# The first sequence's strided attention: 18 rows a block on TensorE, three residues a group, two groups written at once

## Chip, core and metric

One NeuronCore of a Trainium2 chip (trn2). The metric is the device time of one execution in microseconds. The profiler gives, beside that, the span from the first to the last instruction and one row per instruction.

## What is computed

Strided and local causal attention over 4 sequences of 576 positions with 8 heads of 64, then a gated FFN and a maxout FFN over the 2304 tokens, all in fp32:

```python
rel = pos[:, None] - pos[None, :]
mask_local = (rel >= 0) & (rel < 32)                                     # heads 0 to 3
mask_strided = (rel >= 0) & (pos[None, :] % 32 == pos[:, None] % 32)     # heads 4 to 7
attn = softmax(where(mask, q @ k.T / 8, -1e9)) @ v                       # 4 x 8 x 576 x 64
x = attn as 2304 x 512
x = (silu(x @ w_gate) * (x @ w_val)) @ w_out                             # d_ff 1536
out = max(x @ w1, x @ w2, x @ w3) @ w_out2                               # d_ff 768
```

## The kernel before

**Tiling.** A row is 32 tokens, so a sequence has `NI` = 18 rows and the four have 72. They are cut into five chunks of 15, 15, 14, 14 and 14 rows (`ROWS`). The gated FFN runs a chunk at a time: for each of 12 slices f of d_ff a gate product (`emit_gate`), a value product (`emit_val`) and, one slot later, the output product (`emit_out`). A product takes three TensorE passes over a high and a low part (L503 to L505, 480 columns), and the output product of chunk 0 is one fp32 matmul (L549). `x` of a chunk, high and low part, lies in SBUF (`x_tile(c)`, L345 and L346 write it). The maxout FFN follows from about 560 us on.

**Attention.** In local attention a block of two rows sees itself and the row before. In strided attention a position sees only positions of its own residue modulo 32, so one residue of one sequence is a causal attention of 18 by 18. The kernel does it in two ways. On TensorE (`strided_block`): `ON_PE` holds, for a sequence, how many rows are done so and how many residues make a group; a group of 4 residues by 16 rows is a masked attention of 64 by 64, and a `Block` holds two groups. On VectorE or GpSimd (`Unit`): all 32 residues and 4 heads lie on 128 partitions, and a row's scores are an elementwise product with K (L415) and a sum (L418), its output a product with V (L437) and a sum (L440).

**A block** is loaded with three DMAs (L287 to L289), then scores (L299, or L303 outside the opening), a VectorE scan per group (L311), L314, exps on ScalarE (L316), L319 to L321, transposes (L326), their copy out of PSUM (L329 on ScalarE, for every third block L331 on VectorE), the product with V (L340), and, for each piece that `dst` yields, a write of the high part by ScalarE (L345) and of the low part by VectorE (L346). A strided block's `dst` yields one piece for each group and each chunk that its rows touch.

**The opening.** Before the FFN starts, the four strided blocks of the first sequence and four local blocks (rows 0 to 15) are done with tiles from the pool of weights (`wpool`, 35 tiles of 128 x 512). Loads of raw weights come after the blocks with index 2 and 7 (`RAW_AT`). Then eight steps of weight conversion (`LEADW`) are put out.

**Chunk 0's slots.** Each slot holds three steps of weight conversion: a load of a raw float64 weight (L147, 4 buffers), ScalarE (L158, L159), GpSimd (L160, L161), VectorE (L162, which frees the raw buffer, and L163), and a split into high (L135, ScalarE) and low (L138); value and output weights are also written to DRAM (L176) for the later chunks. `attention_steps(1)` puts the attention of chunk 1 into the same slots: the local blocks of rows 16 to 29, the four strided blocks of the second sequence (rows 0 to 11 of it), and, on VectorE, a unit of rows 16 and 17 of the first sequence, with its loads of K, V and q (L399, L400, L404). Chunk 2's attention, with a unit of rows 12 to 17 of the second sequence on GpSimd, begins three slots before chunk 1.

**Order.** The order on each engine is set at build time by a scheduler that simulates the kernel; every engine and SyncE's queue of DMA issues then run their instructions in that order. `silu` (L523) and exp (L316, L425) use different tables of ScalarE, so a change between them is an `ACT_TABLE_LOAD`.

Of the kernel before, what the change touches and what calls it, by code (L numbers as in the profile page):

```python
# [15 lines left out]
B, H, S, D = 4, 8, 576, 64  # L16
DM, DFF, DFF2 = 512, 1536, 768
NT = B * S
STRIDE = 32
NI = S // STRIDE  # L20

LR = 2
QB = LR * STRIDE
# [14 lines left out]
NC = len(ROWS) - 1  # L38
N = STRIDE * max(ROWS[c + 1] - ROWS[c] for c in range(NC))

ON_PE = [(0, 16, 4), (1, 12, 5)]

EARLY = -(-ROWS[1] // LR)

# [15 lines left out]
def tile_attention_swiglu_maxout(  # L60
# [48 lines left out]
    def f32(ap):  # L109
        return ap.bitcast(F32)  # L110


    cols = [128, KB, KB] + [n * r for _, n, r in ON_PE]
    cst = const.tile([128, sum(cols)], F32, name="cst")
# [3 lines left out]
    def width(c):  # L118
        return STRIDE * (ROWS[c + 1] - ROWS[c])

    def pieces(i0, i1):

        for c in range(NC):
            a, b = max(i0, ROWS[c]), min(i1, ROWS[c + 1])
            if a < b:
                yield c, a - ROWS[c], b - ROWS[c], a - i0
# [110 lines left out]
    def x_tile(c):  # L237
        if c not in xt:
            xt[c] = tuple(x_p.tile([128, NK, N], F32R, name=f"x{p}", tag=f"x{p}{c % 2}") for p in "hl")
        return xt[c]  # L240
# [4 lines left out]
    class Block:  # L245
# [86 lines left out]

        def pv(self):
            ps = self.bank()
            nu = self.nu
            for u in range(nu):
                for h in range(4):
                    a, j = divmod(h, 2)
                    m = (2 * u + a) * 128 + j * QB
                    nc.tensor.matmul(  # L340
                        ps[j * D:(j + 1) * D, (a * nu + u) * QB:(a * nu + u + 1) * QB], self.v[:, u, h],
                        self.pt[:, m:m + QB], start=True, stop=True,
                    )
            for hi, lo, src in self.dst(ps[:, :2 * nu * QB].rearrange("p (a m) -> p a m", a=2)):
                nc.scalar.activation(hi, src, AF.Copy)  # L345
                nc.vector.tensor_tensor(lo, src, f32(hi), ALU.subtract)  # L346

    def local_block(g, early=False):


        def dst(src):
            for c, i0, i1, o in pieces(LR * g[0], LR * (g[-1] + 1)):
                t, w = slice(i0 * STRIDE, i1 * STRIDE), slice(o * STRIDE, (o + i1 - i0) * STRIDE)
                xh, xl = x_tile(c)
                yield xh[:, 0:2, t], xl[:, 0:2, t], src[:, :, w]

        src = (earq if early else locq, lock, locv)
        return Block(src, (g[0] if early else g[0] - EARLY, g[0]), KB, [mask[0 if n % (NI // LR) == 0 else 1] for n in g], dst, early)

    def strided_block(srcs, b, g, early=False):  # L360

        _, rows, nr = ON_PE[b]

        def dst(src):
            for u, n in enumerate(g):
                r0 = min(n * nr, STRIDE - nr)
                su = src[:, :, u * QB:u * QB + nr * rows].rearrange("p a (r i) -> p a r i", i=rows)
                for c, i0, i1, o in pieces(b * NI, b * NI + rows):
                    def part(t):
                        t = t[:, 2:4, :width(c)].rearrange("p a (i r) -> p a r i", r=STRIDE)  # L370
                        return t[:, :, r0:r0 + nr, i0:i1]

                    xh, xl = x_tile(c)
                    yield part(xh), part(xl), su[:, :, :, o:o + i1 - i0]

        return Block(srcs, (g[0], g[0]), rows * nr, [smask[b]] * len(g), dst, early)

    def pairs(ns):
        ns = list(ns)
        return [ns[i:i + 2] for i in range(0, len(ns), 2)]  # L380

    class Unit:
# [28 lines left out]
        def qk(self, r, eng):  # L411
            i = self.i0 + r
            pr = pr_p.tile([128, NI * D], F32, name="pr")
            pv = pr[:, :(i + 1) * D].rearrange("p (j d) -> p j d", d=D)
            eng.tensor_tensor(  # L415
                pv, self.k[:, 0:i + 1, :], self.q[:, r:r + 1, :].to_broadcast([128, i + 1, D]), ALU.mult
            )
            nc.vector.tensor_reduce(self.sc[:, r, 0:i + 1], pv, AX.X, ALU.add)  # L418
# [14 lines left out]
        def pv(self, r, eng):  # L433
            i = self.i0 + r
            pr = pr_p.tile([128, NI * D], F32, name="pr")
            pv = pr[:, :(i + 1) * D].rearrange("p (d j) -> p d j", d=D)
            eng.tensor_tensor(  # L437
                pv, self.v[:, :, 0:i + 1], self.sc[:, r:r + 1, 0:i + 1].to_broadcast([128, D, i + 1]), ALU.mult
            )
            nc.vector.tensor_reduce(self.o[:, r], pv, AX.X, ALU.add)  # L440
# [20 lines left out]
    def attention_steps(c):  # L461
# [4 lines left out]
        blocks = [local_block(g) for g in pairs(g for g in range(-(-a // LR), -(-b // LR)) if g >= EARLY)]  # L466
        if a <= NI < b and len(ON_PE) > 1:
            blocks += [strided_block((st1q, st1k, st1v), 1, g) for g in pairs(range(-(-STRIDE // ON_PE[1][2])))]
        at = [0, 0, 4, 4, 8] if len(blocks) < 6 else [0, 0, 2, 2, 4, 4, 6, 6, 8]
# [6 lines left out]
        units = []  # L476
        on_pe = {n: rows for n, rows, _ in ON_PE}
        i = a
# [39 lines left out]
    def emit_gate(c, f):  # L518
        n = width(c)
        ps = gv.tile([128, 512], F32, name="ps_g", tag="gv")  # L520
        linear(ps[:, :n], wt["g", f], xt[c], n)
        t = h_p.tile([128, N], F32, name="ht", tag="ht" if c or f % 2 else "hh")[:, :n]
        nc.scalar.activation(t, ps[:, :n], AF.Silu)  # L523
        return t
# [227 lines left out]
    if True:  # L752
        blocks = [strided_block((st0q, st0k, st0v), 0, g, True) for g in pairs(range(-(-STRIDE // ON_PE[0][2])))]
        blocks += [local_block(g, True) for g in pairs(range(EARLY))]
# [30 lines left out]
        for s, (c, f) in enumerate(slots):  # L785
# [6 lines left out]
            t = emit_gate(c, f)  # L792
# [172 lines left out]
```

## Time and profile before

| | us |
|---|---|
| median of 3 runs | 852.14 |
| lowest, highest | 848.91, 855.87 |
| the profiled execution | 850.72 |
| its span, first to last instruction | 848.9 |
| TensorE busy in the span | 808.7 (95%) |
| VectorE, ScalarE, GpSimd busy | 519.3, 374.4, 408.7 |
| mean granted clock of TensorE | 0.986 of full |

Busy time is a mean over stages with different limits. A timeline row gives start, length, engine, line and, in brackets, how long the engine stood idle before it and what released it. PE is TensorE's matmul, DVE VectorE, ACT ScalarE, POOL GpSimd, SPq the queue of SyncE.

### The profile page before, as it was taken

The page shows a single profiled execution, that of the slowest core. Times are in us where ns is not written, and L with a number is a line of the kernel's source. Part 1 is how long each engine was busy: PE and PEld are TensorE (multiplying, and loading weights), DVE is VectorE, ACT ScalarE, POOL GpSimd, SP SyncE. Part 2 cuts the span into 40 slices and gives each one's busy share as a digit, 9 for nine tenths or more (in the row PEclk, how much of TensorE's full clock was granted, in tenths as well). Part 3 has the DMA queues.
Part 4 walks back from the last instruction along what each step waited for, and adds up shares of the span by engine and source line. Part 5 has one row for each costly group of instructions (what it writes and reads, how often), then busy time and mean ns, then how long its engine had stood idle before and what let it go on. Part 6 is the DMA issues. An engine that isn't in the chain of part 4 may idle for free.

```text
span 848.9 us, 12625 instructions
## 1 busy us (share of the span) xinstructions
PE 808.7 (95%) x4392; PEld 712.2 (84%) x4392; DVE 519.3 (61%) x1028; ACT 374.4 (44%) x844; POOL 408.7 (48%) x355
## 2 busy tenths in 40 slices
PE   4699988989999999999998999999999999999997
PEld 3577665768888899989887999999999899989986
DVE  3889977886576778846889552543644254524340
ACT  4987677653545353645243233432244123512220
POOL 0586566876477869746788444430313021302110
PEclk9799998999999999999999999999999999999999
DMA  8779688986766699868677997579766385654502
GB/s 231 237 237 363 202 273 294 361 261 215 246 201 217 220 311 313 297 194 274 205 226 212 350 300 271 169 291 407 252 234 217 129 284 215 220 190 147 212 1 75
DMA packets 73915, 202.72 MB, mean 239 GB/s; under 512 B 8716, under 2 KB 38472, under 8 KB 70268
## 3 DMA queue, kind: packets, MB, share of 16 engines
q1 hardware_dynamic: 73852, 201.92, 69.8%
q8 instruction: 35, 0.57, 0.3%
q14 instruction: 28, 0.23, 0.1%
HBM read 160.21 MB, written 41.68 MB: 238 GB/s over the span
## 4 chain that ended last, share of the span: by engine, by line
PE 63%; DVE 7%; POOL 3%; DMA 2%; issue 2%; ACT 2%; SPq 0%; DVEq 0%; ACTq 0%; POOLq 0%
PE ps_a L611 13%; PE ps_z L684 8%; PE ps_c L611 7%; PE ps_v L503 3%; PE ps_g L503 3%; PE ps_y L505 3%; PE ps_v L505 3%; PE ps_g L504 3%; PE ps_b L611 3%; PE ps_v L504 3%; PE ps_y L504 3%; PE ps_y L503 3%; PE ps_g L505 3%; POOL pr L415 1%; DMA wr<-wsdr 1%
## 5 line engine op out<-in xcount | busy, mean ns | idle before, releaser
L138 POOL TENSOR_TENSOR hl<-t,hh 128x384 fp32r<-128x384 f32 x36 | 37.6, 1047 | 207.5 <-ACT hh L135 160.4
L503 PE MATMUL ps_g<-xh,wh_g 128*128 128x448 f32 (+1 forms) x240 | 94.4, 394 | 10.2 <-ACT ht L523 8.1
L611 PE MATMUL ps_a<-yhT,wr 128*128 128x384 f32 x324 | 94.4, 338 | 0.6 <-ACT s L625 0.6
L503 PE MATMUL ps_v<-xh,w_v 128*128 128x448 f32 (+1 forms) x240 | 90.5, 377 | 3.5 <-DVE ht L530 3.3
L138 POOL TENSOR_TENSOR hl<-ht,hh 128x448 fp32r<-128x448 f32 (+1 forms) x48 | 60.1, 1253 | 68.1 <-ACT hh L135 60.7
L504 PE MATMUL ps_g<-xl,wh_g 128*128 128x448 f32 (+1 forms) x240 | 90.7, 378 | 0.9 <-DVE xl L346 0.9
L505 PE MATMUL ps_g<-xh,wl_g 128*128 128x448 f32 (+1 forms) x240 | 90.2, 376 | 0.0
L505 PE MATMUL ps_v<-xh,w_v 128*128 128x448 f32 (+1 forms) x240 | 89.5, 373 | 0.0
L504 PE MATMUL ps_v<-xl,w_v 128*128 128x448 f32 (+1 forms) x240 | 89.2, 372 | 0.0
L625 ACT ACTIVATE s<-ps_a 128x384 f32<-128x384 f32 x81 | 39.4, 490 | 98.4 <-PE ps_a L611 98.2
L437 POOL TENSOR_TENSOR pr<-stv,stsc 128x832 f32<-128x832 f32 (+17 forms) x42 | 67.5, 1625 | 29.2 <-DVE stsc L430 13.4
L415 POOL TENSOR_TENSOR pr<-stk,stq 128x832 f32<-128x832 f32 (+17 forms) x42 | 70.9, 1708 | 9.0 <-DVE sto L440 7.3
L505 PE MATMUL ps_y<-hh,w_o 128*128 128x448 f32 (+1 forms) x192 | 71.4, 372 | 0.0
L504 PE MATMUL ps_y<-hl,w_o 128*128 128x448 f32 (+1 forms) x192 | 71.2, 371 | 0.0
L160 POOL TENSOR_SCALAR raw<-raw 128x512 f32<-128x512 f32 x60 | 54.1, 902 | 33.4 <-ACT w L158 15.9
L503 PE MATMUL ps_y<-hh,w_o 128*128 128x448 f32 (+1 forms) x192 | 68.2, 374 | 0.0
L135 ACT ACTIVATE hh<-ht 128x448 fp32r<-128x448 f32 (+1 forms) x48 | 28.0, 584 | 88.4 <-DVE ht L530 88.4
L684 PE MATMUL ps_z<-wo2t,hh 128*128 128x512 f32 x216 | 64.8, 392 | 0.9 <-ACT osb L693 0.7
L530 DVE TENSOR_TENSOR ht<-ps_v,ht 128x448 f32<-128x448 f32 (+1 forms) x60 | 37.9, 631 | 41.9 <-PE ps_v L505 25.8
L503 PEld LDWEIGHTS ps_g<-xh,wh_g 128*128 128x128 f32 x240 | 45.8, 191 | 18.6 <-ACT ht L523 10.0
L611 PEld LDWEIGHTS ps_a<-yhT,wr 128*128 128x128 f32 x324 | 59.7, 188 | 1.6 <-ACT s L625 1.0
L163 DVE CUSTOM_DVE_ANT_0 w<-w,q 128x1024 uint16<-128x1024 uint16 x60 | 54.1, 902 | 1.7
(138 smaller groups left out, 1982.4 us busy)
## 6 DMA issues: line engine op xcount, KB each, us to landing
wr<-wsdr SPq DMA_DIRECT2D x27, 1792.0 KB, 7.5
raw<-in_w_dram SPq DMA_DIRECT2D x60, 512.0 KB, 5.3
w_v<-wvdr SPq DMA_DIRECT2D x48, 512.0 KB, 4.7
w_o<-wodr SPq DMA_DIRECT2D x48, 512.0 KB, 4.8
wsdr<-whi SPq DMA_DIRECT2D x27, 256.0 KB, 4.0
wvdr<-w_v SPq DMA_DIRECT2D x12, 512.0 KB, 4.5
wodr<-w_o SPq DMA_DIRECT2D x12, 512.0 KB, 5.8
wsdr<-w SPq DMA_DIRECT2D x18, 256.0 KB, 4.1
```

The lines of the kernel that those rows point to most:

```text
L138: return a.ins, lo_eng.tensor_tensor(lo, src, f32(hi), ALU.subtract).ins
L160: nc.gpsimd.tensor_scalar(f32(hi), f32(hi), -0.0, 1.0, ALU.mult, ALU.mult)
L163: nc.vector.tensor_tensor(w, w, q, ALU.add)
L415: eng.tensor_tensor(pv, self.k[:, 0:i + 1, :], self.q[:, r:r + 1, :].to_broadcast([128, i + 1, D]), ALU.mult)
L437: eng.tensor_tensor(pv, self.v[:, :, 0:i + 1], self.sc[:, r:r + 1, 0:i + 1].to_broadcast([128, D, i + 1]), ALU.mult)
L503: nc.tensor.matmul(ps, wh, xh, start=first, stop=False)
L504: nc.tensor.matmul(ps, wh, xl, start=False, stop=False)
L505: nc.tensor.matmul(ps, wl, xh, start=False, stop=last)
L530: m = nc.vector.tensor_tensor(t, ps[:, :n], t, ALU.mult).ins
L611: nc.tensor.matmul(ps, wts[:, c, a, ks], y[k][b], start=first and k == q == 0, stop=k == 1 and q == 2, skip_group_check=True,)
L625: nc.scalar.activation(s, self.a, AF.Copy)
L684: nc.tensor.matmul(z[j], a[:, ts], w[:, f, b], start=f == q == 0, stop=f == NF2 - 1 and q == 2)
```

## The change

`ON_PE` gives the first sequence 18 rows in place of 16, and 3 residues a group in place of 4. Its strided part is then 11 groups of 54 positions: five blocks of two groups and one of a single group, whose three residues, 29 to 31, begin with the last residue of the group before. The product with V packs the two groups of a block side by side without the unused columns (54 and not 64 apart), and `dst` writes two groups as one piece where their residues adjoin. `attention_steps`, unchanged, makes units only of rows that `ON_PE` does not name.

```diff
-ON_PE = [(0, 16, 4), (1, 12, 5)]
+ON_PE = [(0, NI, 3), (1, 12, 5)]
...
         def pv(self):
             ps = self.bank()
-            nu = self.nu
+            nu, nq = self.nu, min(QB, self.nk)
             for u in range(nu):
                 for h in range(4):
                     a, j = divmod(h, 2)
                     m = (2 * u + a) * 128 + j * QB
+                    o = (a * nu + u) * nq
                     nc.tensor.matmul(
-                        ps[j * D:(j + 1) * D, (a * nu + u) * QB:(a * nu + u + 1) * QB], self.v[:, u, h],
-                        self.pt[:, m:m + QB], start=True, stop=True,
+                        ps[j * D:(j + 1) * D, o:o + nq], self.v[:, u, h], self.pt[:, m:m + nq], start=True, stop=True,
                     )
-            for hi, lo, src in self.dst(ps[:, :2 * nu * QB].rearrange("p (a m) -> p a m", a=2)):
+            for hi, lo, src in self.dst(ps[:, :2 * nu * nq].rearrange("p (a m) -> p a m", a=2)):
...
         def dst(src):
-            for u, n in enumerate(g):
-                r0 = min(n * nr, STRIDE - nr)
-                su = src[:, :, u * QB:u * QB + nr * rows].rearrange("p a (r i) -> p a r i", i=rows)
+            r0s = [min(n * nr, STRIDE - nr) for n in g]
+            runs = [(r0s[0], len(g))] if r0s[-1] == r0s[0] + nr * (len(g) - 1) else [(r0, 1) for r0 in r0s]
+            u = 0
+            for r0, m in runs:
+                su = src[:, :, u * nr * rows:(u + m) * nr * rows].rearrange("p a (r i) -> p a r i", i=rows)
+                u += m
                 for c, i0, i1, o in pieces(b * NI, b * NI + rows):
                     def part(t):
                         t = t[:, 2:4, :width(c)].rearrange("p a (i r) -> p a r i", r=STRIDE)
-                        return t[:, :, r0:r0 + nr, i0:i1]
+                        return t[:, :, r0:r0 + m * nr, i0:i1]
```

## Rows read from the trace of the kernel before

**Rows 1.** Stages: length, busy us of PE PEld DVE ACT POOL, clock, DMA share, GB/s
```profile
8.00:20.00 12.00, 7.13 (x79) 5.70 (x77) 5.08 (x51) 7.46 (x41) 0.61 (x1) 1.00 0.99 257
20.00:43.00 23.00, 15.98 (x204) 13.33 (x203) 20.70 (x85) 19.92 (x67) 11.42 (x14) 0.78 0.74 239
48.00:79.00 31.00, 31.00 (x159) 23.12 (x159) 27.52 (x50) 21.77 (x41) 23.26 (x22) 1.00 0.89 299
79.00:103.00 24.00, 23.95 (x116) 17.13 (x116) 23.86 (x36) 17.59 (x36) 13.13 (x14) 1.00 0.70 240
137.00:148.00 11.00, 8.46 (x21) 4.84 (x20) 8.26 (x22) 8.44 (x20) 7.14 (x7) 0.69 0.94 313
148.00:185.00 37.00, 37.00 (x182) 28.00 (x181) 30.18 (x61) 20.42 (x41) 29.11 (x16) 1.00 0.97 340
```

**Rows 2.** Timeline of TensorE: start, length, line, out<-in, count, idle before it
```profile
56.94 3.38 PE L549 MATMUL ps_y<-ht,w 128*128 128x480 f32 x8
...
108.15 0.46 PE L503 MATMUL ps_g<-xh,wh_g 128*128 128x480 f32 x1
...
109.31 0.99 PE L303 MATMUL ps_a<-loct 128*128 128x60 f32 x8
...
121.56 0.49 PE L503 MATMUL ps_g<-xh,wh_g 128*128 128x480 f32 x1 [3.29 <-ACT ht L523]
...
140.34 1.88 PE L303 MATMUL ps_a<-loct 128*128 128x60 f32 x8 [2.54 <-DVE w L163]
142.01 6.04 PE L549 MATMUL ps_y<-ht,w 128*128 128x480 f32 x8
...
188.61 0.77 PE L503 MATMUL ps_g<-xh,wh_g 128*128 128x480 f32 x1 [3.17 <-ACT ht L523]
```

**Rows 3.** VectorE in 79:103, grouped by line: busy us, mean ns, idle before
```profile
L437 DVE TENSOR_TENSOR pr<-stv,stsc 128x1088 f32<-128x1088 f32 (+1 forms) x2 | 3.0, 1556 | 0.0
L440 DVE TENSOR_REDUCE sto<-pr 128x64 f32<-128x1088 f32 (+1 forms) x2 | 2.6, 1304 | 0.0
L418 DVE TENSOR_REDUCE stsc<-pr 128x17 f32<-128x1088 f32 (+1 forms) x2 | 2.6, 1310 | 0.0
L415 DVE TENSOR_TENSOR pr<-stk,stq 128x1088 f32<-128x1088 f32 (+1 forms) x2 | 2.5, 1310 | 0.0
```

**Rows 4.** Timeline of VectorE: low halves of gate and of value weights
```profile
107.25 0.94 DVE L138 TENSOR_TENSOR wl_g<-w,wh_g 128x512 fp32r<-128x512 f32 x1
...
132.69 0.82 DVE L138 TENSOR_TENSOR w_v<-w,w_v 128x512 fp32r<-128x512 f32 x1 [0.20 <-ACT w_v L135]
```

**Rows 5.** Timeline of SyncE's issues of DMAs
```profile
107.03 1.15 SPq L147 DMA_DIRECT2D raw<-in_w_dram  x2
...
133.53 0.33 SPq L176 DMA_DIRECT2D wvdr<-w_v  x1
133.96 0.38 SPq L287 DMA_DIRECT2D loct<-in_st1q_dram  x1
```

**Rows 6.** Timeline of ScalarE: a table load, a raw weight, the silu
```profile
91.69 1.28 ACT L425 ACT_TABLE_LOAD   x1
...
112.16 0.68 ACT L158 ACTIVATE w<-raw 128x512 f32<-128x512 f32 x1 [3.26 <-DMA raw<-in_w_dram]
...
120.94 0.57 ACT L523 ACTIVATE ht<-ps_g 128x480 f32<-128x480 f32 x1
```

**Rows 7.** ScalarE in 0:43, grouped by line and shape: busy us, mean ns, idle before
```profile
L316 ACT ACTIVATE sme<-sme,state 128x64 f32<-128x64 f32 x16 | 5.3, 335 | 9.8 <-DVE state L314 9.8
L345 ACT ACTIVATE xh<-ps_a 128x120 fp32r<-128x120 f32 x8 | 3.0, 377 | 0.0
L329 ACT ACTIVATE qe<-ps_a 64x512 f32<-64x512 f32 x3 | 1.8, 599 | 0.7 <-PE ps_a L326 0.7
```

**Rows 8.** DMA issues in 133:143: kind, count, KB each, us to landing
```profile
loct<-in_st1k_dram SPq DMA_DIRECT2D x1, 120.0 KB, 5.8
loct<-in_st1k_dram SPq DMA_DIRECT2D x1, 60.0 KB, 6.3
```

**Rows 9.** Timelines of GpSimd and ScalarE: the second sequence's unit
```profile
162.05 10.09 POOL L415 TENSOR_TENSOR pr<-stk,stq 128x960 f32<-128x960 f32 x4
174.17 0.29 ACT L425 ACTIVATE stsc<-stsc 128x108 f32<-128x108 f32 x1 [4.54 <-DVE stsc L424]
```

## The prediction

> **What bounds the kernel now.** I read the table of stages first, then the timeline of TensorE inside the stages where it stands still, and then, for each standstill, the engine that TensorE waited for. The table says that TensorE is the bound from 48 us on: busy 31.00 of 31 us and 37.00 of 37 us in two of the stages shown, at full clock [rows 1]. Two kinds of time are not bound by it. The opening to 43 us is one: first loads (DMA share 0.99 in 8:20), then VectorE and ScalarE (20.70 and 19.92 of 23 us). The other is a few standstills in the first chunk of the gated FFN: 3.29 us ahead of 121.56, 2.54 us ahead of 140.34, and 3.17 us ahead of 188.61 [rows 2]. So the change must be priced in two places: what it adds to the opening, and whether what it removes ends a standstill. VectorE work taken away anywhere else is worth nothing, as TensorE sets the pace.
>
> **What the change removes.** Rows 16 and 17 of the first sequence were a unit on VectorE: `attention_steps(1)` makes none now, as rows 15 to 17 are on TensorE and rows 18 to 29 were already. In 79:103 that unit is two products with K (2.5 us), two sums (2.6), two products with V (3.0), two sums (2.6) [rows 3]: 10.7 us, without the small operations of its softmax. VectorE was busy 23.86 of those 24 us [rows 1]. TensorE was busy 23.95 of them, so 10.7 us of VectorE are not 10.7 us of time. What they cost is seen later: the weights' conversion (L162, L163, L138) runs on the same engine behind them. The low half of gate weights number 7 is made from 107.25 to 108.19 [rows 4]; TensorE starts on that gate at 108.15 [rows 2], so the reserve is used up there. The loads of raw weights wait for L162 to free their buffer. One is issued only at 107.03 [rows 5], ScalarE sits idle 3.26 us for it until 112.16 [rows 6], does the conversion, then the exps of a strided block between two table loads, and only at 120.94 the silu that TensorE has been waiting for since 118.3 [rows 2, 6]. Without the unit that load is due some 10 us earlier, the idle 3.26 us of ScalarE go, the silu comes at about 117.7, and the standstill of 3.29 us with it. Bounds: 0 if another wait fills it, 3.3 at most.
>
> The second standstill, ahead of the scores at 140.34, follows the same way. Their load was issued at 133.96, behind a write of converted weights that SyncE could issue only at 133.53 [rows 5]. That write waits for VectorE's L138, which ends at 133.51 [rows 4]. Keys of a block of that kind take 5.8 us to land when issued in 133:143 [rows 8], which brings these, the second of the three loads, to about 140. With the conversion ahead, the write is out of the way and the load goes some 2.4 us earlier, when its buffer is free: a gain of 2.4 to 2.5 us, and 0 if SyncE still stands behind something. After that standstill TensorE's granted clock is 0.69 on the mean of 137:148 [rows 1], part of the stage at the lower level of 1.2 GHz: eight output matmuls take 6.04 us where they take 3.38 at 2.4 GHz, and eight score matmuls 1.88 where they take 0.99 [rows 2]. That is 2.66 + 0.89 = 3.5 us more, which goes if the standstill goes. What is late next there is nothing that the rows show: 148:185 is full.
>
> The unit's loads go too: 576 KB twice and 64 KB, in a stage with a DMA share of 0.89 (48:79) [rows 1]. I count nothing for them, since TensorE hides them. So do I with the table load of the unit's exp on ScalarE (1.28 us [rows 6]) and the one back to silu.
>
> **What it adds in the opening.** Groups of 3 residues by 18 rows (54 columns of 64) instead of 4 by 16: 11 groups for 8, so five pairs and a single for four pairs. Loads: a pair was 3 x 128 KB by its tiles; now 128 + 108 + 108 = 344 KB, and the single half, so 5.5 x 344 = 1892 KB for 1536, +356 KB = 0.365 MB. At the 257 GB/s of 8:20 [rows 1] that is 1.4 us; the local blocks come that much later. A raw weight that was loaded after the last block is now ahead of the last two local blocks (the list of places is 2 and 7): 512 KB, 0.52 MB, 2.0 us more for those two. SyncE issues six loads more, at the pace at which the transfers drain anyway. Exps: six groups more at 0.335 us = 2.0 us; ScalarE is busy 7.46 of 12 us in 8:20 [rows 1, 7], so they fit into the time that the loads take. Evictions of the transposed weights: the rule that gives every third to VectorE sends one and a half more to ScalarE, 0.60 us each = 0.9 us, and these fall after 20 us, where ScalarE is busy 87% and is on the path.
>
> Output evictions: four blocks wrote two groups by two chunks, 16 pairs of instructions; now six blocks write two chunks, 12 pairs, of 180 and 36 columns for 120 and 8. The instruction of 120 columns takes ScalarE 0.377 us [rows 7]; four pairs fewer are at most 1.5 us less there, overlapped, and the ten longer ones eat that up: 0. VectorE gets six scans of a group of scores and two blocks' small operations more, in the stretch of the loads, where it is busy 5.08 of 12 us [rows 1]: 0. The first conversions find 1 free tile of 35 and not 3 (three tiles per strided block, 34 in use), and take the first block's as it is done.
>
> The opening: 1.4 + 0.9 = +2.3 us. From below 0, if the loads' extra time only pushes weight conversions that nobody needs yet (seven pairs of L158 and L159 run before 43 us, and the first gate and value need two). From above 1.4 + 2.0 + 0.9 = 4.3, if the last local block's load ends the wait. I take 2.3, nearest to the row with ScalarE at 87%.
>
> The single's keys and values are rows of 432 and 1024 bytes. The nearest row is the single block of the second sequence, keys of 60 KB in rows of 480 bytes: 6.3 us to land beside 5.8 for 120 KB in the same stage [rows 8]. So a short row buys no time, nor does it cost much. The Trainium skill, DMA: Bandwidth & Descriptors, section Specifications, gives 512 B as the least transfer for line rate and speaks against the new single block; if its 54 KB of keys went at half rate, an estimate by that page, the opening would be 0.2 us longer and the sum 843.9. The trace of before neither confirms nor excludes a difference of that size.
>
> For the second sequence, writing two groups at once saves three pairs of 120-column instructions, under 1 us, in a stage where TensorE sets the time: 0.
>
> **The sum.** The profiled execution took 850.7 us (span 848.9 and 1.8 around it); the median of the three runs is 852.1, 1.4 higher. 850.7 + 2.3 (opening) - 3.3 (first standstill) - 2.5 - 3.5 (second, and its clock) = 843.7 us, 0.8% less. A ratio within 1% of 1 is what a measurement of this kernel can't well tell from no change.
>
> **The rivals.** (A) The gain is given back at the next bound: 843.7 becomes 851 to 853. GpSimd's unit for rows 12 to 17 of the second sequence has four products in a row, 10.09 us from 162.05, and ScalarE sits 4.54 us in its queue until 174.17 for that unit's softmax, with the silu behind it [rows 9]. If this chain stays where it is, a TensorE that comes 7 us sooner stands for 7 us. For it: the chain that ended last goes through exactly these rows. Against it: the loads that start the unit are behind raw weights on SyncE, so they move with the conversion. (B) The third standstill goes as well, since it too is ScalarE's exps in front of a silu: 3.17 us [rows 2], or up to 3.5 more if the clock fell after it as after the second: 843.7 - 3.2 = 840.5, at best 837.0. Against it: those exps wait for a VectorE operation beside GpSimd's product, which the change doesn't touch. (C) Slower. The order on each engine is planned anew. All four strided blocks of the second sequence put exps between two table loads ahead of a silu; one of them stalled TensorE. If a planned order with more room on VectorE puts the exps of all four ahead of their silu, each costs 3.3 us, and two of them the clock's 3.5 as well: 4 x 3.3 + 2 x 3.5 = 20.2, less the 9.3 that stood there before, with the opening's 2.3: 850.7 + 13.2 = 863.9. It decides from three such standstills on; the rows have one in four.
>
> **How the numbers follow.** Forecast (843.7, own range 841 to 849 by the opening's bounds and half of the second standstill with its clock): 0.50. A: 0.27. B: 0.15. C: 0.08. Range 837 to 855: it takes in B, the forecast and A with the opening's upper bound (852.7 + 2.0), and leaves out C and some of the tails. Faster by over 1% (below 842.2): all of B and some 0.3 of the forecast, 0.30. Slower by over 1% (above 859.2): most of C, 0.07. Within: 0.63.
>
> **What would show it.** The first gate matmul some 2.3 us later than before: the opening. No L415 on VectorE in 79:103, and the low gate weights made several us ahead of their gate: the reserve. No idle of 3 us on TensorE between 110 and 150, and the clock at 1.00 there: the standstills. If the gap is gone and the end is not earlier, look for a wait on a silu near 170: rival A. If there are more gaps on a silu than before: C. The prediction is wrong in its base if the first gate starts over 4.3 us later, or if the conversion is as late as before without the unit.

## The result: 0.97% slower, and the profile after

The changed kernel takes 859.65 us (median of 6 runs, 858.88 to 862.48) beside 852.68 us for the kernel before (6 runs, 848.91 to 855.87): ratio 1.0097, 95% interval 1.0073 to 1.0121. The forecast was 843.7 us, its range 837 to 855. The profiled execution has a span of 858.0 us, before 848.9: +9.1 (by the medians +7.0). In the new file lines behind the changed function are three higher: the silu is L526, VectorE's product of gate and value L533, GpSimd's product with K L418.

The table of stages after (length, busy us of PE, PEld, DVE, ACT, POOL, clock, DMA share, GB/s), to be laid beside [rows 1]:

```profile
8.00:20.00 12.00, 9.07 (x136) 7.14 (x136) 8.57 (x69) 8.85 (x45) 0.91 (x2) 1.00 0.93 283
20.00:43.00 23.00, 16.52 (x190) 13.31 (x189) 19.36 (x75) 20.95 (x68) 12.93 (x15) 0.63 0.77 206
48.00:79.00 31.00, 29.25 (x136) 21.67 (x137) 25.44 (x44) 21.49 (x44) 19.07 (x21) 0.92 0.76 245
79.00:103.00 24.00, 23.88 (x124) 17.46 (x123) 20.06 (x41) 18.95 (x39) 14.25 (x16) 1.00 0.86 281
137.00:148.00 11.00, 10.95 (x49) 7.94 (x48) 7.65 (x11) 6.97 (x13) 5.42 (x8) 1.00 0.98 340
148.00:185.00 37.00, 31.50 (x143) 22.46 (x142) 27.75 (x55) 14.07 (x29) 26.33 (x14) 0.91 0.76 261
```

The forecast's two effects are here: VectorE is busy 20.06 of 24 us in 79:103 instead of 23.86, and 137:148, which was busy 8.46 us at a clock of 0.69, is full at 1.00. But two stages that were full are not now: 48:79 (29.25 of 31, clock 0.92) and 148:185 (31.50 of 37, clock 0.91). The timeline of TensorE after shows what it waited for there:

```profile
44.79 0.48 PE L506 MATMUL ps_g<-xh,wh_g 128*128 128x480 f32 x1 [1.39 <-ACT xh L345]
...
47.95 1.09 PE L326 MATMUL ps_a<-cst,sm 128*96 128x128 f32 x4 [2.46 <-DVE sm L321]
...
57.41 0.49 PE L506 MATMUL ps_g<-xh,wh_g 128*128 128x480 f32 x1 [1.75 <-ACT ht L526]
...
111.16 1.07 PE L303 MATMUL ps_a<-loct 128*128 128x60 f32 x8 [1.72 <-DMA loct<-in_st1k_dram]
...
124.42 0.60 PE L326 MATMUL ps_a<-cst,sm 128*60 128x128 f32 x4 [1.62 <-DVE stat L319]
...
130.94 0.49 PE L506 MATMUL ps_g<-xh,wh_g 128*128 128x480 f32 x1 [0.84 <-ACT ht L526]
...
157.65 0.48 PE L506 MATMUL ps_v<-xh,w_v 128*128 128x480 f32 x1 [3.99 <-DVE ht L533]
...
161.85 1.46 PE L326 MATMUL ps_a<-cst,sm 128*60 128x128 f32 x6 [1.51 <-DVE sm L321]
...
198.94 0.49 PE L506 MATMUL ps_g<-xh,wh_g 128*128 128x480 f32 x1 [2.03 <-ACT ht L526]
```

Of the three standstills of [rows 2] the second is gone, the first is 0.84 us and the third 2.03. New ones stand at 47.95, 57.41, 111.16, 124.42, 161.85 and, the largest, at 157.65.

**Where the 9.1 us are.** A slot (chunk, f) is counted from its first gate matmul to the next one's, read from that timeline. Late against before: slot (0,0) +2.03 (44.79 for 42.76), (0,1) +6.23, (0,9) +9.50, (0,10) +2.98, (0,11) +11.13, (2,0) +8.07. It stays at +8.05 to (3,9), is +10.53 at (3,10), and the second FFN brings it to +9.1. Beside the 2.03 us of the opening the loss is made in three places: 4.20 us in slot (0,0), 3.27 between (0,1) and (0,9), and 8.15 in slot (0,10), which takes 17.48 us for 9.33. Slot (0,9) gains 6.52, and some 3.1 are made up between (0,11) and (2,0). A profile is one execution, and its places scatter: three other kernels below whose VectorE, ScalarE and GpSimd have the changed kernel's order through the opening start their first gate at 44.93, 45.81 and 46.19 us beside its 44.79.

**The end of the opening.** VectorE after:

```profile
45.37 0.39 DVE L346 TENSOR_TENSOR xl<-ps_a,xh 128x256 fp32r<-128x256 f32 x1
45.68 0.68 DVE L162 SCALAR_TENSOR_TENSOR w<-w,raw 128x512 int32<-128x512 int32 x1
46.28 1.62 DVE L321 TENSOR_TENSOR sm<-sm,stat 128x384 f32<-128x384 f32 x1
47.82 0.34 DVE L346 TENSOR_TENSOR xl<-ps_a,xh 128x192 fp32r<-128x192 f32 x1
```

and ScalarE after, ahead of the first silu:

```profile
54.85 0.63 ACT L135 ACTIVATE w_v<-w 128x512 fp32r<-128x512 f32 x1
55.49 1.28 ACT L526 ACT_TABLE_LOAD   x1
56.79 0.57 ACT L526 ACTIVATE ht<-ps_g 128x480 f32<-128x480 f32 x1
```

The high part of x was complete at 44.74; its last low part is made at 47.82, because a conversion and the softmax of a block that nobody needs yet come first in VectorE's order. The softmax's product (L321) takes 1.62 us, beside a low half that GpSimd makes from 45.91 to 47.48. In TensorE's own order the transposes of that same block come next, so it stands 2.46 us for the softmax, then runs at 0.40 us a matmul until 52.8 (granted clock 0.50 in 47.95:52.80, the lower level), and then waits for a silu behind exps, a weight and a table load.

**Slot (0,10).** GpSimd, then VectorE, after:

```profile
149.62 4.91 POOL L418 TENSOR_TENSOR pr<-stk,stq 128x832 f32<-128x832 f32 x2
154.49 1.26 POOL L138 TENSOR_TENSOR w_o<-w,w_o 128x512 fp32r<-128x512 f32 x1
```

```profile
150.81 0.21 DVE L311 CUSTOM_DVE_ANT_0 sm<-ps_a,cst 128x60 f32<-128x60 f32 x1
...
150.95 1.61 DVE L163 CUSTOM_DVE_ANT_0 w<-w,q 128x1024 uint16<-128x1024 uint16 x1
152.49 2.13 DVE L314 TENSOR_SCALAR stat<-stat 128x4 f32<-128x4 f32 x2
154.54 1.76 DVE L162 SCALAR_TENSOR_TENSOR w<-w,raw 128x512 int32<-128x512 int32 x1
...
156.94 0.65 DVE L533 TENSOR_TENSOR ht<-ps_v,ht 128x480 f32<-128x480 f32 x1
```

The next value's matmuls need the bank that L533 empties. VectorE's L163, L314 and L162 take some 5.5 us instead of 1.6: the first two stand beside GpSimd's two products with K, the third beside the low half (L138) that GpSimd makes behind them. Each ends just behind the GpSimd instruction that it met: L163 at 152.56, 0.55 us behind the first product, the first L314 at 154.55, 0.02 us behind the second, and L162 at 156.30, 0.55 us behind the low half. The standstill at 161.85 comes the same way: ahead of the L321 that TensorE waits for, VectorE's L138 takes 2.60 us from 158.78, beside the next product. The two standstills are 5.5 of the 8.15 us; behind the first the granted clock is 0.60 in 158.50:167.00.

In the kernel before the same product started at 153.25. SyncE issued its load of K at 143.90, and now at 141.43; in both it stands directly behind a raw weight (before, then after):

```profile
143.48 0.37 SPq L147 DMA_DIRECT2D raw<-in_w_dram  x1
143.90 0.75 SPq L399 DMA_DIRECT2D stk<-in_strd_dram  x1
```

```profile
140.96 0.38 SPq L147 DMA_DIRECT2D raw<-in_w_dram  x1
141.43 0.72 SPq L402 DMA_DIRECT2D stk<-in_strd_dram  x1
```

So it moved with the conversion of the weights. The buffer of K and V, which the removed unit used as well, is not the reason: before, that unit's last product with V ended at 98.4, some 45 us ahead of the load. Two runs below show that the unit's removal brings the load forward. TensorE is 2.98 us later, GpSimd 3.6 us earlier, and the two meet. Before, the collision hit other instructions (VectorE before):

```profile
153.63 2.13 DVE L138 TENSOR_TENSOR w_v<-w,w_v 128x512 fp32r<-128x512 f32 x1 [0.88 <-ACT w_v L135]
155.68 2.58 DVE L162 SCALAR_TENSOR_TENSOR w<-w,raw 128x512 int32<-128x512 int32 x1
158.17 0.65 DVE L530 TENSOR_TENSOR ht<-ps_v,ht 128x480 f32<-128x480 f32 x1
```

There L530 came while TensorE was still on the next gate, and nothing waited.

### The profile page after: what moved, and what is told of

Its sections match the earlier page's. It is cut to its first block, busy times and chain, and to the rows that moved or that the text cites. A ratio compares the mean times of both kernels' runs of the same rounds, so it can differ in the third digit from the quotient of the medians.

```text
span 858.0 us, 12740 instructions
## 1 busy us (share of the span) xinstructions
PE 814.3 (95%) x4444; PEld 716.9 (84%) x4444; DVE 511.4 (60%) x1024; ACT 378.2 (44%) x848; POOL 401.1 (47%) x355
## 4 chain that ended last, share of the span: by engine, by line
PE 69%; DVE 4%; issue 2%; DMA 2%; POOL 2%; ACT 1%; SPq 0%; ACTq 0%; DVEq 0%
PE ps_a L614 13%; PE ps_z L687 8%; PE ps_c L614 6%; PE ps_y L506 4%; PE ps_v L506 4%; PE ps_v L508 4%; PE ps_v L507 4%; PE ps_y L508 4%; PE ps_g L507 4%; PE ps_y L507 4%; PE ps_g L508 4%; PE ps_g L506 4%; PE ps_b L614 3%; DMA wr<-wsdr 1%; POOL pr L440 1%
## 5 line engine op out<-in xcount | busy, mean ns | idle before, releaser
L138 POOL TENSOR_TENSOR hl<-t,hh 128x384 fp32r<-128x384 f32 x36 | 37.6, 1046 | 207.3 <-ACT hh L135 160.4
L506 PE MATMUL ps_v<-xh,w_v 128*128 128x448 f32 (+1 forms) x240 | 91.5, 381 | 7.3 <-DVE ht L533 7.3
L138 POOL TENSOR_TENSOR hl<-ht,hh 128x448 fp32r<-128x448 f32 (+1 forms) x48 | 60.4, 1257 | 71.3 <-ACT hh L135 65.5
L508 PE MATMUL ps_v<-xh,w_v 128*128 128x448 f32 (+1 forms) x240 | 91.1, 380 | 0.0
L418 POOL TENSOR_TENSOR pr<-stk,stq 128x832 f32<-128x832 f32 (+17 forms) x42 | 69.7, 1678 | 12.2 <-DVE sto L443 6.9
L533 DVE TENSOR_TENSOR ht<-ps_v,ht 128x448 f32<-128x448 f32 (+1 forms) x60 | 37.9, 632 | 57.8 <-PE ps_v L508 43.0
L160 POOL TENSOR_SCALAR raw<-raw 128x512 f32<-128x512 f32 x60 | 49.2, 821 | 32.1 <-issue 16.3
L163 DVE CUSTOM_DVE_ANT_0 w<-w,q 128x1024 uint16<-128x1024 uint16 x60 | 56.7, 944 | 2.1
```

The lines of the kernel that those rows point to most:

```text
L138: return a.ins, lo_eng.tensor_tensor(lo, src, f32(hi), ALU.subtract).ins
L160: nc.gpsimd.tensor_scalar(f32(hi), f32(hi), -0.0, 1.0, ALU.mult, ALU.mult)
L163: nc.vector.tensor_tensor(w, w, q, ALU.add)
L418: eng.tensor_tensor(pv, self.k[:, 0:i + 1, :], self.q[:, r:r + 1, :].to_broadcast([128, i + 1, D]), ALU.mult)
L506: nc.tensor.matmul(ps, wh, xh, start=first, stop=False)
L508: nc.tensor.matmul(ps, wl, xh, start=False, stop=last)
```

## The experiments

Two theories stood against each other. O: the change saves what it takes from VectorE, and the loss comes of the order on each engine, which is planned anew for every edit. L: the work that the change adds costs the time. O's ranges are wide (846 to 860 us in one case), so a time inside them says little for O; what these runs can do is exclude L. Each ratio is to the kernel before on the same chip.

### The parts of the change

**The writes alone.** The changed kernel with `ON_PE = [(0, 16, 4), (1, 12, 5)]`.

> The changed kernel's writes (two groups of a block at once, groups packed side by side) with the rows and groups of before: 16 rows, 4 residues a group, the unit on VectorE. Work differs by some tenths of a microsecond. Theory O (what costs is the order that is planned anew: standstills of TensorE move to other places): the time may be anywhere from 846 to 860 us, and the standstills of the first chunk stand in other slots than before. Rival L (what costs is the load that the opening takes on): nothing is added here, so 852.7 +- 2 us.

Measured: 856.86 us, ratio 1.0054 (1.0030 to 1.0078). Slot (0,0) +1.79, (0,1) +6.08, with a wait of 2.63 us for the first silu. The same instructions within a few, and 0.5% slower.

**The unit left out of the kernel before.** Rows 16 and 17 of the first sequence are not computed; their x is set to zero.

```
-            if i % NI < on_pe.get(i // NI, 0):
+            if i % NI < on_pe.get(i // NI, 0) or i < NI:
```

> The kernel before without the unit of rows 16 and 17 of the first sequence: it is left out, its x is set to zero by GpSimd ahead of the opening. The prediction's terms say -3.3 - 2.5 - 3.5 us: 852.7 - 9.3 = 843.4 us. Rival L says the same, 843 us, because the opening is that of before. Theory O says that the two standstills named go and others come: 845 to 857 us, with at least one new standstill of over 1.5 us in the first chunk.

Measured: 845.98 us, ratio 0.9938 (0.9920 to 0.9957): 5.4 us less, not 9.3. The opening is that of before (slot (0,1) -0.79). The standstill of 3.29 us is gone; at 134.95 one of 1.24 and at 147.78 one of 2.36 us stand in the place of the second. The load of K goes at 135.39 for 143.90, and GpSimd's product starts at 147.00 for 153.25.

**The unit computed as well in the changed kernel** (`min(rows, 16)` in the rows that need no unit).

> The changed kernel, but the unit on VectorE still computes rows 16 and 17 of the first sequence a second time. If the prediction's gain from the unit's removal is real in the changed kernel, this is 859.7 + 9.3 = 869 us. Rival L: the opening alone costs what was measured and more, 866 to 870 us. Theory O: the unit's 10.7 us of VectorE weigh less than the order, 855 to 866 us.

Measured: 863.20 us, ratio 1.0140 (1.0108 to 1.0172), 3.5 us above the changed kernel. The load of K goes at 150.93 for the changed kernel's 141.43, the product starts at 161.05, and slot (0,10) takes 9.00 us.

**The raw weight back behind the blocks.** `RAW_AT = [2, 9]` in the changed kernel.

> The changed kernel with the second raw weight loaded after the last block, as before, instead of ahead of the last two local blocks; the order on the engines is the same as in the changed kernel, only SyncE's queue differs. Rival L, with the prediction's upper bound: the last two local blocks land 2.0 us earlier and the first gate starts up to 2 us earlier: 857.6 us. Theory O: the order of the engines is the same, so are the standstills, 859.7 +- 1 us.

Measured: 860.41 us, ratio 1.0103 (1.0070 to 1.0136). The moved load costs nothing: VectorE, ScalarE and GpSimd keep the changed kernel's order up to 297 us, and the first gate comes at 46.53 us, not earlier than its 44.79.

**The groups alone.** The kernel before with `(0, NI, 3)`, writes as they were.

> The kernel before with the 18 rows in groups of 3 residues alone; the writes stay as they were, one group at a time. The prediction's sum (the groups carry all of the gain and of the opening's cost): ratio 0.992. If the two parts' costs add up (writes alone 1.0054, both 1.0097): 1.0043. Theory O (no part has a price of its own, the planned order decides): anything from 0.995 to 1.013, with a first gate matmul within 2.5 us of the changed kernel's 44.79 and the difference made in the slots after it.

Measured: 858.89 us, ratio 1.0082 (1.0057 to 1.0106). Slot (0,0) starts 6.36 us late here, at 49.12 and so outside what was expected, (0,1) 7.50; slot (0,10) has the standstill too (3.47 us). Writes alone and groups alone add to 1.0136, together they are 1.0097: the parts have no prices that add, and the 0.992 of the prediction's sum was missed.

### The order alone

Four pairs of kernels follow. In each the kernel before and the changed one get the same rule for the order and nothing else; the work of each stays what it was.

**Lag 5.** `lag = 5` for 4: the opening's transposes five blocks behind the scores.

> The kernel before with the transposes of the opening issued five blocks behind the scores instead of four. Not an instruction more or less: only the planned order is another. Theory O: the time moves by several us all the same, either way (0.4% to 1.5%), with TensorE's standstills in chunk 0 at other places than 121.56, 140.34 and 188.61. Rival L: within 1.5 us of the kernel before, with the three standstills where they were.

> The changed kernel with the opening's transposes five blocks behind the scores: the partner of the kernel before with the same lag (ratio 1.011). The two differ in the change alone, and neither has the order that the kernel before had. Theory O (the change itself gains what it takes from VectorE, and the loss is that of leaving the order of before): faster than its partner by 4 to 8 us, ratio 1.001 to 1.006. Rival L (the change itself costs time): slower than its partner by the 8 us that it costs at lag 4, ratio 1.018 to 1.022.

**Lag 3.**

> The kernel before with the opening's transposes three blocks behind the scores instead of four: the same work, another planned order. Theory O: slower than before by 0.4% to 1.3%, as with lag 5 (1.011) and with chunk 1 a slot later (1.0063); slot (0,1) at 55 to 59 where before has 51.18. Rival: the kernel before is one order among many that are alike, and the ratio is within 0.997 to 1.003.

> The changed kernel with lag 3, the partner of the kernel before with lag 3. Theory O (away from before's own order the change gains what it takes from VectorE): faster than its partner by 2 to 7 us. Rival L (the change itself costs time, and lag 5 was chance): slower than its partner by 2 us or more.

**Chunk 1's attention a slot later**: `fill.setdefault(i + 1 if c == 1 else ...`.

> The kernel before with the attention of chunk 1 one FFN slot later. The work is the same, and so is the order on each engine up to the third silu. Theory O: the opening and the slots to (0,3) are as before (42.8, 51.2, 60.5), and the time moves by 0.3% to 1.2%, by standstills at new places after slot (0,4). Rival: the order matters only at the end of the opening, and the time is within 1.5 us of before.

> The changed kernel with chunk 1's attention one slot later, the partner of the kernel before with the same shift (1.0063). That partner keeps before's opening (slot (0,1) at 52.27), this one the changed kernel's (57.4). Theory O with the loss in the opening's end: slot (0,1) at 57 to 58, so 5 us behind the partner there, and from (0,1) to (2,0) 2 to 7 us less than the partner's 233.5: 0.999 to 1.004 of the partner, ratio 1.004 to 1.011. Rival L: 1.012 or more.

**The end of the opening tied**: VectorE's part of the eight reserve conversions, and the scans of the FFN's blocks, planned behind the last low part of x.

```
+            if behind[0]:
+                tied.enter_context(tc.issue_after(early_lo[0]))
             nc.vector.scalar_tensor_tensor(w, w, 3, hi, ALU.logical_shift_left, ALU.bitwise_xor)
```

> The changed kernel with VectorE's part of the eight reserve conversions, and the first scans of the FFN's blocks, planned behind the last low part of x. The work is the same. Theory O, with its place (x's last low part is made at 47.82 though its high part is there at 44.74, since conversions and a stretched product stand ahead of it on VectorE): the low part ends within 1 us of the high part, TensorE does not stand 2.46 us at 47.95, nor 1.75 us for the first silu; slot (0,1) starts 3 to 4.5 us earlier than 57.41. The time then is 853 to 857 if the slots after it are as in the changed kernel; with every later instruction planned anew they may lose it again. Rival L: slot (0,1) no earlier than 56.5.

> The kernel before with the rule for VectorE's order at the end of the opening that took the changed kernel from 859.65 to 856.63: the partner of that one. Theory O: again slower than before, 1.004 to 1.012, and within 5 us of its partner, more likely above it, since the two rows on VectorE are still to be paid. Rival (the rule is good for both): within 1.5 us of before or faster.

Measured, in us (slot times from the timelines of TensorE):

| order | before: time, ratio | changed: time, ratio | slot (0,0) starts | slot (0,1) starts | (0,1) to (2,0) |
|---|---|---|---|---|---|
| as it was | 852.68, 1 | 859.65, 1.0097 | 42.76, 44.79 | 51.18, 57.41 | 229.84, 231.68 |
| lag 5 | 861.12, 1.0110 (1.0066 to 1.0155) | 855.86, 1.0050 (1.0032 to 1.0068) | 44.43, 48.25 | 56.95, 57.20 | 235.42, 228.06 |
| lag 3 | 858.12, 1.0086 (1.0057 to 1.0115) | 857.83, 1.0081 (1.0053 to 1.0109) | 44.46, 50.67 | 53.46, 60.76 | 234.06, 227.16 |
| chunk 1 later | 857.37, 1.0063 (1.0034 to 1.0093) | 856.32, 1.0066 (1.0038 to 1.0094) | 42.89, 46.19 | 52.27, 58.64 | 233.48, 227.34 |
| opening tied | 862.88, 1.0127 (1.0096 to 1.0157) | 856.63, 1.0061 (1.0037 to 1.0084) | 42.48, 45.82 | 49.46, 52.46 | 241.14, 232.42 |

Three things follow. The kernel before loses 0.6% to 1.3%, some 5 to 11 us, in each of the four other orders, with the same work. With lag 5 its VectorE even shows the picture of the changed kernel, a conversion ahead of the low part:

```profile
44.46 1.00 DVE L163 CUSTOM_DVE_ANT_0 w<-w,q 128x1024 uint16<-128x1024 uint16 x1
45.38 1.09 DVE L138 TENSOR_TENSOR w_v<-w,w_v 128x512 fp32r<-128x512 f32 x1
46.40 0.34 DVE L346 TENSOR_TENSOR xl<-ps_a,xh 128x192 fp32r<-128x192 f32 x1
```

Second, in all four new orders the changed kernel is 6.1 to 8.7 us shorter from (0,1) to (2,0). That the unit alone cost so much is not shown: leaving it out of the kernel before makes this stretch 3.3 us shorter, computing it in the changed kernel as well makes it 3.4 us longer, and the writes alone, with the unit, take 229.13. Third, it starts its first gate 3.3 to 6.2 us later than its partner (2.03 in the old order). What is left is two pairs equal within 1.1 us and two in which the changed kernel is 5 to 6 us ahead (in lag 5 the two intervals overlap slightly). L expected it behind in the three pairs for which it was put on record, and it is behind in none. O missed too: in lag 3 the changed kernel was to be 2 to 7 us ahead and is level with its partner, whose slot (0,1) starts at 53.46 and not at 55 to 59; and the kernel before with the tie came out at 1.0127, above the 1.012 and over 5 us behind its partner.

The tie did at its place what was expected: the low part follows the high part, and slot (0,1) starts at 52.46 for 57.41. Of those 4.95 us the slots up to (0,6) took all back (105.44 for 105.42): new waits, one of 2.78 us on VectorE at 92.29.

**Exps behind the silu.** The changed kernel; the exps of a block may not stand ahead of the silu issued before them.

```
+                if last_silu and not self.early:
+                    tied.enter_context(tc.issue_after(last_silu[0]))
                 for g in range(ng):
                     nc.scalar.activation(
```

> The changed kernel with one rule more for the planned order: the exps of a block in the FFN may not stand ahead of the silu issued before them. The work is the same. Theory O (the planned order costs the time: in the changed kernel the exps of chunk 1's second block and a table load stand ahead of the first silu, and TensorE waits 1.75 us for it at 57.41): the standstill on the silu ahead of slot (0,1) is gone, and the later ones at 130.94 and 198.94 (0.84 and 2.03 us) shrink; ratio to the kernel before 1.003 to 1.007 instead of 1.0097. Rival L (the work added in the opening costs the time, whatever the order): slot (0,1) starts as late as in the changed kernel, ratio 1.009 to 1.012.

Measured: 860.77 us, ratio 1.0114 (1.0066 to 1.0162). The wait for the first silu is 2.82 us and not gone: three conversions stand there in the exps' place. The two later waits shrink as expected (0.56 and 0.85 us), but a new one of 3.81 us for a silu stands at 155.82. Exps ahead of a silu were only what happened to stand there.

### GpSimd's product and slot (0,10)

**A slot later by the program's order.** `(c - 1) * NF + i - (2 if c == 2 else 3)`, for chunk 2 alone.

> The changed kernel with chunk 2's attention, so GpSimd's unit for rows 12 to 17 of the second sequence, one FFN slot later. Theory G (the wait of 3.99 us at 157.65, for VectorE's product of the gate and value, comes of VectorE's small operations standing beside GpSimd's product from 149.62 on, 2.13 us for a pair that takes 0.3): that wait goes and the lower clock after it, 4 to 8 us less than the changed kernel, ratio 1.000 to 1.005. Rival: the collision moves one slot on, and the ratio stays at 1.008 to 1.012.

Measured: 866.94 us, ratio 1.0177 (1.0138 to 1.0216). A miss as a test: VectorE, ScalarE and GpSimd keep the changed kernel's order up to 243 us, so the product stays where it was (150.83 for 149.62), and the standstill is 4.68 us. Chunk 2, which now gets its attention later, loses 6 us more up to (2,5).

**Without the products with K**, and the sums behind them (rows 12 to 17 of the second sequence).

> The changed kernel without the products of queries and keys of GpSimd's unit (rows 12 to 17 of the second sequence) and their sums; the softmax goes over a constant. On VectorE and ScalarE the order up to the place in question is the same. Theory G (the standstill of 3.99 us at 157.65 comes of GpSimd's product from 149.62, beside which VectorE's small operations take 2.13 us for two): VectorE's pair at L314 takes 0.3 us, the product of gate and value on VectorE comes 3 us earlier, the standstill shrinks to under 1.5 us; 4 to 9 us less than the changed kernel, ratio 0.999 to 1.005. Rival (VectorE's and ScalarE's order alone makes the standstill): it stays at 3 us or more, and the time falls by less than 2 us.

Measured: 855.79 us, ratio 1.0056 (1.0032 to 1.0080). A miss too: the products with V moved into the place, VectorE's pair takes 2.04 us, the standstill is 3.89. The 4 us less come later, between (1,1) and (1,6).

**Without any product of that unit**; its output is zero.

> The changed kernel without any product of GpSimd's unit of the second sequence, with K or V, and without their sums (its output is set to zero). VectorE and ScalarE keep their order up to the product of gate and value in question. Theory G: nothing long runs on GpSimd from 149 to 155, VectorE's pair at L314 takes 0.3 us instead of 2.0 to 2.1, and the standstill of 3.99 us at 157.65 falls below 1.5 us. Rival: VectorE's order alone makes it, and it stays at 3 us or more. The time: 853 to 857 in either case, since work is left out after that place too.

Measured: 850.93 us, ratio 0.9993 (0.9972 to 1.0015). GpSimd does nothing from 150.7 to 153.49. VectorE of this kernel:

```profile
152.01 0.68 DVE L163 CUSTOM_DVE_ANT_0 w<-w,q 128x1024 uint16<-128x1024 uint16 x1
152.62 0.23 DVE L314 TENSOR_SCALAR stat<-stat 128x4 f32<-128x4 f32 x2
152.76 0.68 DVE L162 SCALAR_TENSOR_TENSOR w<-w,raw 128x512 int32<-128x512 int32 x1
153.47 0.69 DVE L163 CUSTOM_DVE_ANT_0 w<-w,q 128x1024 uint16<-128x1024 uint16 x1
154.08 0.65 DVE L539 TENSOR_TENSOR ht<-ps_v,ht 128x480 f32<-128x480 f32 x1
```

The order is that of the changed kernel, the durations are short, the standstill is gone, and slot (0,10) takes 10.56 us.

**The unit's loads behind the last write of converted weights**, with nothing left out.

```
-            with tc.issue_after(raw_dma[0].ins):
+            with tc.issue_after(raw_dma[0].ins), tc.issue_after(wr_dma[0]):
```

> The changed kernel with one order more on SyncE: the loads of GpSimd's unit of the second sequence go behind the last write of converted weights, not just behind the last raw load. No work is left out. Theory G (the product beside VectorE's small operations costs slot (0,10) some 7 us, 3.99 of standstill and the rest lower clock): the first product starts behind 158 instead of at 149.62, slot (0,10) takes 10 to 11 us instead of 17.48, and the time is 852 to 855, ratio 1.000 to 1.005. Rival: the later unit is late for its own chunk, TensorE waits for it near 200, and the ratio stays at 1.007 or more.

Measured: 854.58 us, ratio 1.0024 (1.0004 to 1.0044) for the changed kernel's 1.0097. GpSimd of this kernel, then VectorE:

```profile
168.19 8.57 POOL L419 TENSOR_TENSOR pr<-stk,stq 128x832 f32<-128x832 f32 x4 [12.80 <-DMA stq<-in_strd_dram]
```

```profile
152.69 0.23 DVE L315 TENSOR_SCALAR stat<-stat 128x4 f32<-128x4 f32 x2
152.84 0.68 DVE L163 SCALAR_TENSOR_TENSOR w<-w,raw 128x512 int32<-128x512 int32 x1
...
154.16 0.65 DVE L534 TENSOR_TENSOR ht<-ps_v,ht 128x480 f32<-128x480 f32 x1
```

Slot (0,10) takes 11.30 us for 17.48, and up to 157 us VectorE's order is the changed kernel's. From (0,1) to (2,0) the kernel takes 225.64 us, 4.2 less than before and the least of all but those with work left out. Its end of the opening is as bad as the changed kernel's ((0,1) at 58.16). No kernel tried here that computes everything beats the one before.

## Why the prediction was wrong

The sum had +2.3 for the opening, -3.3 and -6.0 for two standstills, and nothing else. In the profiles these places gave +2.03, +3.27 and -6.52, and two places that stood at nothing gave +4.20 (slot (0,0)) and +8.15 (slot (0,10)).

**The reserve: right.** Without the unit conversion is off the path. The low half of gate weights number 7 starts at 101.90, and TensorE comes to that gate at 118.34; before it was 107.25 and 108.15 [rows 2, 4]:

```profile
101.90 0.94 DVE L138 TENSOR_TENSOR wl_g<-w,wh_g 128x512 fp32r<-128x512 f32 x1 [0.76 <-ACT wh_g L135]
```

**First standstill, -3.3: the wait went, the time did not.** It is 0.84 us, but loads of the second sequence's keys are late instead (1.72 us at 111.16, 0.55 at 112.78), a softmax is late at 124.42 (1.62 us), and from (0,1) to (0,9) the changed kernel takes 3.27 us more than before. The first keys' load was issued at 105.31, before at 102.65. In SyncE's new order it stands behind raw weights, the last of which waits until 103.9 for L162 to free its buffer:

```profile
98.82 5.48 SPq L147 DMA_DIRECT2D raw<-in_w_dram  x3
104.36 0.42 SPq L176 DMA_DIRECT2D wodr<-w_o  x1
104.83 0.44 SPq L287 DMA_DIRECT2D loct<-in_st1q_dram  x1
105.31 1.35 SPq L288 DMA_DIRECT2D loct<-in_st1k_dram  x1
```

No run changed that order alone.

**Second standstill and its clock, -6.0: right in number, not by its mechanism.** Slot (0,9) is 6.52 us shorter, and 137:148 is full at full clock. But the load of those keys did not go 2.4 us earlier: it went 2.46 us later (before, then after).

```profile
134.38 1.25 SPq L288 DMA_DIRECT2D loct<-in_st1k_dram  x1
```

```profile
136.84 0.42 SPq L288 DMA_DIRECT2D loct<-in_st1k_dram  x1
```

TensorE no longer waits for it because it reaches slot (0,9) 9.50 us late itself. That part is luck: the 6.52 us win back a delay that the sum did not have.

**"What is late next there is nothing that the rows show": this step failed.** 148:185 was full, and I took that for room. In it stood a product on GpSimd that was harmless only by where it stood. I wrote under rival A that the unit's loads move with the conversion, and did not follow this to the product that starts earlier and to what runs on VectorE beside it. The mechanism is shown: the stretch goes with the products (L314 2.13 to 0.23 us), and with the product later and nothing left out the ratio is 1.0024 and not 1.0097. The Trainium skill, SBUF — State Buffer, section Who interferes with whom, says that VectorE and GpSimd share one pair of ports under an exclusive lock, that a VectorE instruction with two inputs in SBUF contends with a GpSimd instruction that reads SBUF, that one in a two-port mode contends too, and that one with at most one SBUF input, outside those modes, does not. The rows agree: L162 and L163, with two SBUF inputs, are stretched, while L311, which takes one operand from PSUM, keeps its 0.21 us beside the product. So does L533 where it meets one (0.65 us at 166.50, inside a product from 165.30 to 167.78); at 156.94 GpSimd stood idle. The TENSOR_SCALAR has one input in SBUF and is stretched; that it ran in a two-port mode no row shows.

**The opening, +2.3: right in number in the old order, not by its reasons, and too narrow.** +2.03 was measured at the first gate, the low end of what the same opening gave in four kernels (2.03 to 3.43). The 1.4 of the loads and the 0.9 of the evictions were not measured by themselves, and the 2.0 that the moved raw weight put into the upper bound do not show. The writes alone, without the added loads and exps, start it 1.79 us late, and lag 5 with not an instruction more 1.67. The four new pairs give 3.3 to 6.2 for the change, where the upper bound was 4.3. The larger miss is the slot behind it: I ended the opening at the first gate matmul. The low part of x, the lower clock and the first silu come after it, a term that the sum put at nothing, and cost 4.20 us more, here and with the writes alone (4.29).

**Third standstill:** 2.03 for 3.17 us, part of rival B, and worth 1 us.

**The seam, +2.4: not foreseen.** In slot (3,9) both kernels stand still for 3.31 to 3.33 us at the same instruction; the clock fell behind it in one of them (first line before, second after):

```profile
452.00:462.00 10.00, 6.67 (x34) 5.78 (x33) 9.74 (x9) 2.88 (x6) 8.30 (x5) 1.00 0.49 146
```

```profile
460.00:470.00 10.00, 6.69 (x22) 5.59 (x22) 9.74 (x9) 2.87 (x6) 8.30 (x5) 0.66 0.35 109
```

Over all profiled kernels that slot takes from 11.06 us (the raw weight moved) to 13.93 (writes alone), with the same standstill, and variants of both kernels have it short and long, so this part is not shown to be the change's.

**Rival A** did not come: between 161.85 and 198.94 TensorE waits for no silu. GpSimd's chain did not stay where it was; it came 3.6 us earlier.

**Rival C** had the right root, an order planned anew, and the wrong mechanism: exps held behind the silus gained nothing. Its chance of 0.08 was the real error of the distribution. Any of four edits without work cost the kernel before 0.6% to 1.3%; so a change that touches the opening should have had most of its chance on "away from this order", some 6 us up, before its own gain was counted. As an estimate from the pairs, 850.7 + 6 + 3 - 7 is 853, inside the range; the collision, 17.48 us for 11.30 in slot (0,10), takes it out.

What stays open: why the order of before is so much better than the four others, beyond its opening's end; and whether a hand-made order would let the change gain 6 to 9 us without the 3 to 6 of the opening.

## What to carry to other kernels

Where a scheduler plans the order on each engine from the whole program, an edit has two effects, its work and a new order; run the old and the new kernel under two or three rules that change the order alone, and compare within the pairs. Follow each freed resource to what starts earlier because of it, and look which instructions of a neighbouring engine run beside that. A stage that is full today says nothing on what it hides.

## What the hardware showed beyond that

A pair of VectorE operations on 128x4 elements and less took 0.23 us alone and 2.04 to 2.13 beside one of GpSimd's products; L163 went from 0.68 to 1.61 beside a product, L162 to 1.76 beside GpSimd's low half L138 and to 2.58 beside a product. Up to 300 us, in both kernels, all 20 instructions of L138, L162, L163, L314 and L319 on VectorE that took over 1.3 us ended at one distance behind the end of a GpSimd instruction that ran beside them: 0.55 us for the first three, 0.02 to 0.03 for the two on 128x4. So a short operation pays as much as a long one: what counts is how much of GpSimd's instruction is still to come. After a standstill of 3.3 us the granted clock was 1.00 in one execution and 0.66 in another, after one of 2.54 us it fell as well [rows 1, 2]: the length of a wait alone did not tell. The new single block's 54 KB of keys landed in 3.1 us beside 4.7 for 108 KB. The prediction had weighed against it the least transfer for line rate in the Trainium skill, DMA: Bandwidth & Descriptors, section Specifications; no penalty of that kind shows in these two numbers.
